# Attention exponentials tied behind the SiLU of their slot in ScalarE's order

## The chip, the cores and the metric

The kernel runs on one core of a Trainium2 chip. The metric is the device time of one execution in microseconds (us); the time of a kernel is the median of its runs. Engines are named as the profile names them: PE is TensorE, ACT is ScalarE, DVE is VectorE, POOL is GpSimd, SP is SyncE, whose queue issues the DMAs.

## The reference

Three layers, all in float32. First an attention with 4 batches, 8 heads, 576 positions and a head size of 64, in which heads 0 to 3 see the last 32 positions (local) and heads 4 to 7 see every 32nd earlier position (strided):

```python
scores = np.where(masks[None], scale * np.matmul(q, k.transpose(0, 1, 3, 2)), -1000000000.0)
attn = np.exp(scores - np.max(scores, axis=-1, keepdims=True))
attn = attn / (np.sum(attn, axis=-1, keepdims=True) + 1e-09)
x = np.matmul(attn, v)               # becomes 2304 tokens x 512
```

Then a gated layer, `y = (silu(x @ w_gate) * (x @ w_val)) @ w_out`, with 1536 inner columns, and at the end `h = max(y @ w1, y @ w2, y @ w3)` with 768 columns and `out = h @ w_out2`.

## The kernel before, in words

The float32 products are made of high and low parts: each operand is split into a rounded part (`hi`) and the rest (`lo`), and three matmuls stand for one product. The split of a value takes one copy (mostly on ACT) and one subtraction (DVE or POOL).

The 2304 tokens are cut into 5 chunks of 480 or 448 tokens, and the gated layer runs chunk after chunk. In each chunk there are 12 slots, one for each 128 inner columns, 60 slots in all, numbered 0 to 59 here. A slot is `emit_gate` (12 matmuls into `ps_g`, then the SiLU on ACT, L523, into `ht`), `emit_val` (12 matmuls into `ps_v`, the multiplication with `ht` on DVE, L530, and from the second chunk on its split into `hh` and `hl`) and, one slot later, `emit_out` (the matmuls into `ps_y`). `ps_g` and `ps_v` share a pool of two PSUM banks (tag `gv`), so the gate matmuls of one slot can begin only when the SiLU of the slot before has read its bank, and the value matmuls only when the multiplication has.

Attention of a chunk is computed while PE works on the chunk before. It comes in two kinds, and both fill `x` of the coming chunk (`xh`, `xl`):

- A `Block` uses PE for its scores (L299, L303). DVE adds the mask and takes the maximum (L311, L314), ACT takes the exponentials, two or four activations each with its row sum (L316), DVE or POOL normalize (L319 to L321), PE transposes (L326), ACT copies (L329), PE multiplies with the values (L340), and ACT and DVE split the result into `x` (L345, L346). A block's `loc` buffer and its two PSUM banks (tag `att`) are free for a later block when this is done; there are two of each.
- A `Unit` (the strided rows that don't go to PE) has its scores on POOL and DVE (`qk`, L415, L418), then a softmax on DVE and one activation on ACT (L425), its product with the values on POOL and DVE (`pv`, L437, L440), a transpose on PE (L447), and the split into `x` (L458, L459). One `stsc` and one `sto` buffer serve all units in turn.

`attention_steps` spreads these steps over the slots, and the loop over slots emits them (`fill`) behind `emit_gate` and `emit_val` of the slot. In the first 8 blocks (`early`) all comes before the first slot. In slots 0 to 43 there are 20 blocks and 10 units. Their exponentials are emitted in slots 0, 2, 4, 6, 9, 13, 21, 25, 33 and 37 (blocks, two in each) and 2, 11, 15, 19, 23, 27, 31, 35, 39 and 43 (units).

The order in which the program emits instructions isn't the order in which an engine gets them. A planner runs a simulated timeline over the program (`schedule_with_timeline_sim=True`), takes for each engine the earliest emitted instruction that is ready there, and so fixes each engine's order; on the chip each engine works through its order without overtaking. `tc.issue_after(ins)` adds an edge, without a semaphore: what is emitted inside it comes behind `ins` in the order of that engine. The kernel uses it at several places already, such as for the conversion steps of later weights (tied behind the multiplication of their slot).

The activation table of ACT holds either the exponential or the SiLU. Where one follows the other in ACT's order, a table load (`ACT_TABLE_LOAD`) stands between them, shown at the line of the activation that needs it. Copy and Abs run with either table.

After slot 59 a second stage (L570 to L700) computes the last two layers; the change doesn't touch it.

Of the kernel before, what the change touches and what calls it, by code (L numbers as in the profile page):

```python
# [11 lines left out]
AF = mybir.ActivationFunctionType  # L12
# [39 lines left out]
SCALE = 1.0 / D ** 0.5  # L52
# [7 lines left out]
def tile_attention_swiglu_maxout(  # L60
# [18 lines left out]
    nc = tc.nc  # L79
# [38 lines left out]
    def width(c):  # L118
        return STRIDE * (ROWS[c + 1] - ROWS[c])
# [125 lines left out]
    class Block:  # L245
# [59 lines left out]
        def softmax(self, norm_eng):  # L305
            sm, mx, sums, ng = self.sm, self.mx, self.sums, 2 * self.nu
            with ExitStack() as tied:
                if early_order[0] is not None and self.early:
                    tied.enter_context(tc.issue_after(early_order[0]))
                for g in range(ng):  # L310
                    nc.vector.tensor_tensor_reduce(  # L311
                        sm[:, g], self.s[:, g], self.masks[g // 2], 1.0, -3.0e38, ALU.add, ALU.max, mx[:, g:g + 1]
                    )
            early_order[0] = nc.vector.tensor_scalar(mx, mx, -SCALE, None, ALU.mult).ins  # L314
            for g in range(ng):
                nc.scalar.activation(  # L316
                    sm[:, g], sm[:, g], AF.Exp, bias=mx[:, g:g + 1], scale=SCALE, accum_out=sums[:, g:g + 1]
                )
            nc.vector.tensor_scalar(sums, sums, 1.0e-9, None, ALU.add)  # L319
            nc.vector.reciprocal(sums, sums)  # L320
            norm_eng.tensor_tensor(sm, sm, sums[:, :, None].to_broadcast([128, ng, self.nk]), ALU.mult)  # L321
# [60 lines left out]
    class Unit:  # L382
# [37 lines left out]
        def softmax(self):  # L420
            sc, n, jn = self.sc, self.n, self.jn
            mx = tiny.tile([128, 6], F32, name="smx")[:, :n]
            nc.vector.tensor_reduce(mx, sc, AX.X, ALU.max)
            nc.vector.tensor_tensor(sc, sc, mx[:, :, None].to_broadcast([128, n, jn]), ALU.subtract)
            nc.scalar.activation(sc, sc, AF.Exp, scale=SCALE)  # L425
            sums = tiny.tile([128, 6], F32, name="ssum")[:, :n]
            nc.vector.tensor_reduce(sums, sc, AX.X, ALU.add)
            nc.vector.tensor_scalar(sums, sums, 1.0e-9, None, ALU.add)
            nc.vector.reciprocal(sums, sums)
            nc.vector.tensor_tensor(sc, sc, sums[:, :, None].to_broadcast([128, n, jn]), ALU.mult)  # L430
            self.o = st_p.tile([128, 6, D], F32, name="sto")
# [75 lines left out]
    def linear(ps, w, x, n):  # L507
        xh, xl = x
        for k in range(NK):
            ks = slice(k * 128, (k + 1) * 128)  # L510
            product(ps, w[0][:, ks], w[1][:, ks], xh[:, k, :n], xl[:, k, :n], k == 0, k == NK - 1)

    hs = {}

    last_val = []
    yacc = {}

    def emit_gate(c, f):
        n = width(c)
        ps = gv.tile([128, 512], F32, name="ps_g", tag="gv")  # L520
        linear(ps[:, :n], wt["g", f], xt[c], n)
        t = h_p.tile([128, N], F32, name="ht", tag="ht" if c or f % 2 else "hh")[:, :n]
        nc.scalar.activation(t, ps[:, :n], AF.Silu)  # L523
        return t

    def emit_val(c, f, t):
# [225 lines left out]
    if True:  # L752
# [32 lines left out]
        for s, (c, f) in enumerate(slots):  # L785
# [4 lines left out]
            if work:  # L790
                weight_step()
            t = emit_gate(c, f)
            if work:
                weight_step()
# [170 lines left out]
```

## Time and profile before

| what | value |
|---|---|
| runs | 848.91, 852.14, 855.87 us; median 852.14 us |
| the profiled execution's own time | 850.72 us |
| span in its profile (first to last instruction) | 848.9 us |
| mean granted TensorE clock | 0.986 of full speed |
| PE busy | 808.7 us, 95% of the span |
| ACT busy | 374.4 us, 44% |
| DVE and POOL busy | 519.3 us (61%) and 408.7 us (48%) |

A row of the timeline has the start, the duration, the engine, the line, the operation with its output and inputs, and in brackets the engine's idle time before it and what ended that. The SiLUs of the 60 slots run in the order of the slots, so the n-th SiLU of the timeline belongs to slot n - 1, and an exponential's place among them can be read off. A row of the windows view gives, for a stretch, its length and the busy time of each engine with the number of instructions, then the granted clock (1.00 is 2.4 GHz, half of it 1.2 GHz) and the DMA's share and rate.

### The profile page before, as it was taken

What the parts mean: (1) busy time and instruction counts of PE and PEld (TensorE: products, weight loads), DVE (VectorE), ACT (ScalarE), POOL (GpSimd) and SP (SyncE); (2) the same over time, 40 slices, a digit from 0 to 9 for tenths busy, and PEclk for the clock granted to TensorE, in tenths of its full rate; (3) what the DMA queues carried; (4) which work ended last, traced back from release to release, by engine and by line L of the source; (5) the groups of instructions that cost most, each with busy time, mean ns of one, the idle gap of its engine ahead of it and who ended that gap; (6) DMA issues with size and microseconds to landing.
All of it is one profiled execution on the core that took longest, in us unless ns stands there. A gap on an engine that the chain in (4) does not pass through costs nothing.

```text
span 848.9 us, 12625 instructions
## 1 busy us (share of the span) xinstructions
PE 808.7 (95%) x4392; PEld 712.2 (84%) x4392; DVE 519.3 (61%) x1028; ACT 374.4 (44%) x844; POOL 408.7 (48%) x355
## 2 busy tenths in 40 slices
PE   4699988989999999999998999999999999999997
PEld 3577665768888899989887999999999899989986
DVE  3889977886576778846889552543644254524340
ACT  4987677653545353645243233432244123512220
POOL 0586566876477869746788444430313021302110
PEclk9799998999999999999999999999999999999999
DMA  8779688986766699868677997579766385654502
GB/s 231 237 237 363 202 273 294 361 261 215 246 201 217 220 311 313 297 194 274 205 226 212 350 300 271 169 291 407 252 234 217 129 284 215 220 190 147 212 1 75
DMA packets 73915, 202.72 MB, mean 239 GB/s; under 512 B 8716, under 2 KB 38472, under 8 KB 70268
## 3 DMA queue, kind: packets, MB, share of 16 engines
q1 hardware_dynamic: 73852, 201.92, 69.8%
q8 instruction: 35, 0.57, 0.3%
q14 instruction: 28, 0.23, 0.1%
HBM read 160.21 MB, written 41.68 MB: 238 GB/s over the span
## 4 chain that ended last, share of the span: by engine, by line
PE 63%; DVE 7%; POOL 3%; DMA 2%; issue 2%; ACT 2%; SPq 0%; DVEq 0%; ACTq 0%; POOLq 0%
PE ps_a L611 13%; PE ps_z L684 8%; PE ps_c L611 7%; PE ps_v L503 3%; PE ps_g L503 3%; PE ps_y L505 3%; PE ps_v L505 3%; PE ps_g L504 3%; PE ps_b L611 3%; PE ps_v L504 3%; PE ps_y L504 3%; PE ps_y L503 3%; PE ps_g L505 3%; POOL pr L415 1%; DMA wr<-wsdr 1%
## 5 line engine op out<-in xcount | busy, mean ns | idle before, releaser
L138 POOL TENSOR_TENSOR hl<-t,hh 128x384 fp32r<-128x384 f32 x36 | 37.6, 1047 | 207.5 <-ACT hh L135 160.4
L503 PE MATMUL ps_g<-xh,wh_g 128*128 128x448 f32 (+1 forms) x240 | 94.4, 394 | 10.2 <-ACT ht L523 8.1
L611 PE MATMUL ps_a<-yhT,wr 128*128 128x384 f32 x324 | 94.4, 338 | 0.6 <-ACT s L625 0.6
L503 PE MATMUL ps_v<-xh,w_v 128*128 128x448 f32 (+1 forms) x240 | 90.5, 377 | 3.5 <-DVE ht L530 3.3
L138 POOL TENSOR_TENSOR hl<-ht,hh 128x448 fp32r<-128x448 f32 (+1 forms) x48 | 60.1, 1253 | 68.1 <-ACT hh L135 60.7
L504 PE MATMUL ps_g<-xl,wh_g 128*128 128x448 f32 (+1 forms) x240 | 90.7, 378 | 0.9 <-DVE xl L346 0.9
L505 PE MATMUL ps_g<-xh,wl_g 128*128 128x448 f32 (+1 forms) x240 | 90.2, 376 | 0.0
L505 PE MATMUL ps_v<-xh,w_v 128*128 128x448 f32 (+1 forms) x240 | 89.5, 373 | 0.0
L504 PE MATMUL ps_v<-xl,w_v 128*128 128x448 f32 (+1 forms) x240 | 89.2, 372 | 0.0
L625 ACT ACTIVATE s<-ps_a 128x384 f32<-128x384 f32 x81 | 39.4, 490 | 98.4 <-PE ps_a L611 98.2
L437 POOL TENSOR_TENSOR pr<-stv,stsc 128x832 f32<-128x832 f32 (+17 forms) x42 | 67.5, 1625 | 29.2 <-DVE stsc L430 13.4
L415 POOL TENSOR_TENSOR pr<-stk,stq 128x832 f32<-128x832 f32 (+17 forms) x42 | 70.9, 1708 | 9.0 <-DVE sto L440 7.3
L505 PE MATMUL ps_y<-hh,w_o 128*128 128x448 f32 (+1 forms) x192 | 71.4, 372 | 0.0
L504 PE MATMUL ps_y<-hl,w_o 128*128 128x448 f32 (+1 forms) x192 | 71.2, 371 | 0.0
L160 POOL TENSOR_SCALAR raw<-raw 128x512 f32<-128x512 f32 x60 | 54.1, 902 | 33.4 <-ACT w L158 15.9
L503 PE MATMUL ps_y<-hh,w_o 128*128 128x448 f32 (+1 forms) x192 | 68.2, 374 | 0.0
L135 ACT ACTIVATE hh<-ht 128x448 fp32r<-128x448 f32 (+1 forms) x48 | 28.0, 584 | 88.4 <-DVE ht L530 88.4
L684 PE MATMUL ps_z<-wo2t,hh 128*128 128x512 f32 x216 | 64.8, 392 | 0.9 <-ACT osb L693 0.7
L530 DVE TENSOR_TENSOR ht<-ps_v,ht 128x448 f32<-128x448 f32 (+1 forms) x60 | 37.9, 631 | 41.9 <-PE ps_v L505 25.8
L503 PEld LDWEIGHTS ps_g<-xh,wh_g 128*128 128x128 f32 x240 | 45.8, 191 | 18.6 <-ACT ht L523 10.0
L611 PEld LDWEIGHTS ps_a<-yhT,wr 128*128 128x128 f32 x324 | 59.7, 188 | 1.6 <-ACT s L625 1.0
L163 DVE CUSTOM_DVE_ANT_0 w<-w,q 128x1024 uint16<-128x1024 uint16 x60 | 54.1, 902 | 1.7
(138 smaller groups left out, 1982.4 us busy)
## 6 DMA issues: line engine op xcount, KB each, us to landing
wr<-wsdr SPq DMA_DIRECT2D x27, 1792.0 KB, 7.5
raw<-in_w_dram SPq DMA_DIRECT2D x60, 512.0 KB, 5.3
w_v<-wvdr SPq DMA_DIRECT2D x48, 512.0 KB, 4.7
w_o<-wodr SPq DMA_DIRECT2D x48, 512.0 KB, 4.8
wsdr<-whi SPq DMA_DIRECT2D x27, 256.0 KB, 4.0
wvdr<-w_v SPq DMA_DIRECT2D x12, 512.0 KB, 4.5
wodr<-w_o SPq DMA_DIRECT2D x12, 512.0 KB, 5.8
wsdr<-w SPq DMA_DIRECT2D x18, 256.0 KB, 4.1
```

The lines of the kernel that those rows point to most:

```text
L138: return a.ins, lo_eng.tensor_tensor(lo, src, f32(hi), ALU.subtract).ins
L160: nc.gpsimd.tensor_scalar(f32(hi), f32(hi), -0.0, 1.0, ALU.mult, ALU.mult)
L163: nc.vector.tensor_tensor(w, w, q, ALU.add)
L415: eng.tensor_tensor(pv, self.k[:, 0:i + 1, :], self.q[:, r:r + 1, :].to_broadcast([128, i + 1, D]), ALU.mult)
L437: eng.tensor_tensor(pv, self.v[:, :, 0:i + 1], self.sc[:, r:r + 1, 0:i + 1].to_broadcast([128, D, i + 1]), ALU.mult)
L503: nc.tensor.matmul(ps, wh, xh, start=first, stop=False)
L504: nc.tensor.matmul(ps, wh, xl, start=False, stop=False)
L505: nc.tensor.matmul(ps, wl, xh, start=False, stop=last)
L530: m = nc.vector.tensor_tensor(t, ps[:, :n], t, ALU.mult).ins
L611: nc.tensor.matmul(ps, wts[:, c, a, ks], y[k][b], start=first and k == q == 0, stop=k == 1 and q == 2, skip_group_check=True,)
L625: nc.scalar.activation(s, self.a, AF.Copy)
L684: nc.tensor.matmul(z[j], a[:, ts], w[:, f, b], start=f == q == 0, stop=f == NF2 - 1 and q == 2)
```

## The change

`emit_gate` keeps its SiLU in the list `silu`, and the exponentials of blocks and units go through `exp`, which ties them behind it. For the early blocks the list is empty, and nothing is tied.

```diff
@@ Block.softmax
             for g in range(ng):
-                nc.scalar.activation(
+                exp(
                     sm[:, g], sm[:, g], AF.Exp, bias=mx[:, g:g + 1], scale=SCALE, accum_out=sums[:, g:g + 1]
                 )
@@ Unit.softmax
-            nc.scalar.activation(sc, sc, AF.Exp, scale=SCALE)
+            exp(sc, sc, AF.Exp, scale=SCALE)
@@
     last_val = []
+    silu = []
+
+    def exp(*args, **kw):
+        with ExitStack() as tied:
+            for ins in silu:
+                tied.enter_context(tc.issue_after(ins))
+            nc.scalar.activation(*args, **kw)
+
@@ emit_gate
-        nc.scalar.activation(t, ps[:, :n], AF.Silu)
+        silu[:] = [nc.scalar.activation(t, ps[:, :n], AF.Silu).ins]
         return t
```

## Rows read from the trace of the kernel before

**Rows 1.** The page's parts 1 and 2: busy time of engines; granted clock by slices

```profile
PE 808.7 (95%) x4392; PEld 712.2 (84%) x4392; DVE 519.3 (61%) x1028; ACT 374.4 (44%) x844; POOL 408.7 (48%) x355
...
PEclk9799998999999999999999999999999999999999
```

**Rows 2.** Windows view of all engines, three stretches of the gated layer

```profile
42.00:60.00 18.00, 16.32 (x64) 12.31 (x64) 17.61 (x35) 14.24 (x39) 14.43 (x12) 0.91 0.73 237
...
402.00:440.00 38.00, 37.27 (x205) 33.26 (x203) 30.56 (x34) 12.57 (x29) 32.59 (x21) 1.00 0.70 228
440.00:480.00 40.00, 35.77 (x177) 32.42 (x178) 29.63 (x36) 14.25 (x27) 25.95 (x18) 1.00 0.77 255
```

**Rows 3.** Timeline of PE: the three waits for a SiLU

```profile
121.56 0.49 PE L503 MATMUL ps_g<-xh,wh_g 128*128 128x480 f32 x1 [3.29 <-ACT ht L523]
...
188.61 0.77 PE L503 MATMUL ps_g<-xh,wh_g 128*128 128x480 f32 x1 [3.17 <-ACT ht L523]
...
440.90 0.47 PE L503 MATMUL ps_g<-xh,wh_g 128*128 128x448 f32 x1 [1.63 <-ACT ht L523]
```

**Rows 4.** Timeline of ACT around slots 0 and 1

```profile
43.13 0.36 ACT L316 ACTIVATE sm<-sm,stat 128x96 f32<-128x96 f32 x1
...
45.64 0.36 ACT L316 ACTIVATE sm<-sm,stat 128x96 f32<-128x96 f32 x1
...
46.73 1.28 ACT L523 ACT_TABLE_LOAD   x1
48.65 0.57 ACT L523 ACTIVATE ht<-ps_g 128x480 f32<-128x480 f32 x1 [0.63 <-PE ps_g L505]
...
54.09 0.57 ACT L523 ACTIVATE ht<-ps_g 128x480 f32<-128x480 f32 x1
```

**Rows 5.** Timeline of ACT: exponentials of slots 23 and 39, and the SiLUs of 22, 23, 39

```profile
262.33 0.25 ACT L425 ACTIVATE stsc<-stsc 128x48 f32<-128x48 f32 x1
...
268.97 0.57 ACT L523 ACTIVATE ht<-ps_g 128x480 f32<-128x480 f32 x1
...
274.01 0.57 ACT L523 ACTIVATE ht<-ps_g 128x480 f32<-128x480 f32 x1 [1.90 <-PE ps_g L505]
...
390.09 0.27 ACT L425 ACTIVATE stsc<-stsc 128x72 f32<-128x72 f32 x1
...
404.63 0.55 ACT L523 ACTIVATE ht<-ps_g 128x448 f32<-128x448 f32 x1 [1.78 <-PE ps_g L505]
```

**Rows 6.** Groups of ACT's instructions by line: the table loads

```profile
L523 ACT ACT_TABLE_LOAD x17 | 21.8, 1283 | 2.4 <-PE ps_g L505 2.1
...
L425 ACT ACT_TABLE_LOAD x10 | 12.8, 1283 | 9.0 <-DVE stsc L424 8.8
...
L316 ACT ACT_TABLE_LOAD x7 | 9.0, 1283 | 0.8 <-PEq L952 0.7
```

**Rows 7.** Timeline of PE: gate matmuls of slots 2 and 12, and of slot 48

```profile
60.51 0.48 PE L503 MATMUL ps_g<-xh,wh_g 128*128 128x480 f32 x1
...
172.70 0.75 PE L503 MATMUL ps_g<-xh,wh_g 128*128 128x480 f32 x1
...
477.45 0.36 PE L503 MATMUL ps_g<-xh,wh_g 128*128 128x448 f32 x1
```

**Rows 8.** Timeline of POOL: first products with the values of slot 39's unit

```profile
391.47 2.53 POOL L437 TENSOR_TENSOR pr<-stv,stsc 128x448 f32<-128x448 f32 x2 [4.50 <-DVE stsc L430]
...
406.91 2.89 POOL L437 TENSOR_TENSOR pr<-stv,stsc 128x576 f32<-128x576 f32 x2 [3.58 <-DVE sto L440]
```

**Rows 9.** Timeline of DVE: last parts of x for the second and the fifth chunk

```profile
168.36 0.40 DVE L346 TENSOR_TENSOR xl<-ps_a,xh 128x120 fp32r<-128x120 f32 x1
...
472.63 0.35 DVE L459 TENSOR_TENSOR xl<-ps_a,xh 64x192 fp32r<-64x192 f32 x1 [0.39 <-ACT xh L458]
```

**Rows 10.** Windows view of PE alone (length, busy, clock, DMA), behind the wait at 188

```profile
185.00:190.00 5.00, 1.83 (x7) 0.82 0.47 172
190.00:195.00 5.00, 5.00 (x21) 0.84 0.01 3
```

## Prediction

> **What bounds the kernel now.** I read the page's busy times first. PE is busy for 808.7 of 848.9 us, ACT for 374.4, and the granted clock is below full in a few slices only [rows 1]. PE sets the time, and a change in ACT's order is worth what it does to PE's gaps. The windows view says where these are: in the stretch from 42 to 60 us PE is busy for 16.32 of 18, from 402 to 440 for 37.27 of 38, from 440 to 480 for 35.77 of 40 [rows 2]. Then I looked in PE's timeline for waits whose releaser is the SiLU, since that is the instruction the change protects. There are three in the gated layer, of 3.29, 3.17 and 1.63 us, 8.09 in all [rows 3]. Last I compared ACT's order with the slots from which the exponentials are emitted, which tells what the tie can move at all.
>
> **What the tie moves.** Thirty batches of exponentials are tied (20 blocks, 10 units). ACT's order is the planner's order, so a batch that already stands behind its SiLU meets the new edge for nothing. By the timeline 24 of the 30 do; most blocks of the first chunk even run two or three SiLUs late. Six stand too early. The two blocks of slot 0 (8 activations, 43.13 to 46.00) come ahead of SiLU 0 at 48.65 [rows 4]. Four units do too: that of slot 23 runs at 262.33, ahead of SiLU 22, where SiLU 23 is at 274.01; that of slot 39 runs at 390.09 and SiLU 39 at 404.63 [rows 5]; those of slots 27 and 35 repeat the pattern, two and three SiLUs early. None of the three waits of PE stands behind one of these six: the exponentials ahead of the SiLUs of slots 7 and 13, at which PE waited 3.29 and 3.17, were emitted in slots 4 and 9, so the tie permits that order. I expect no direct gain.
>
> **Table loads.** One load takes 1283 ns, and there are 17 + 10 + 7 = 34 [rows 6]. The blocks of slot 0 still use the table of the early blocks; behind SiLU 0 they need a load to the exponential and one back: two more. The units of slots 23, 27 and 39 share their table period with the blocks of slots 21, 25 and 37; behind their own SiLU they stand alone: two more each. The unit of slot 35 had a pair to itself and keeps it. So 34 becomes 42, and ACT gains 8 x 1.283 = 10.3 us of 374. ACT isn't the bound, so only the place of each pair matters.
>
> **Slot 0.** Between SiLU 0 and SiLU 1 now come 8 activations (45.64 + 0.36 - 43.13 = 2.9 us) and two loads (2.6), 5.4 in all. SiLU 1 ends at 54.66 today, and the gate matmuls that need its bank start at 60.51 [rows 4, 7]: 5.85 us of cover, by PE's value and output matmuls between. The 5.4 fits, and 2.9 us of ACT's time ahead of SiLU 0 come free, so I take 0. If that cover weren't there it would cost 5.4. A gain here I leave out: ACT's vacated time lies ahead of SiLU 0, which waits for PE itself (0.63 [rows 4]). Behind the batch wait, on DVE, the row sums' reciprocals and the normalizing, then PE's transposes; through the two `loc` buffers so do SP's three loads of each block of slot 2. The exponentials start at about 48.65 + 0.57 + 1.28 = 50.5 instead of 43.13: 7.4 us late.
>
> The Trainium skill, "ScalarE: Activation LUTs", section "What ACT_TABLE_LOAD costs", puts a drain of about 1380 ns beside each load, 2.66 us a switch, and its section on table sets advises to do all calls of one set together, the opposite of this change. The trace doesn't agree: the load at 46.73 is 1.28 long and ends at 48.01, and the 0.63 from there to the SiLU is a wait for PE [rows 4]. By the page's figure the stretch ahead of SiLU 1 would be 5.4 + 2 x 1.38 = 8.2, over the cover of 5.85 by 2.3, and the sum would be that much higher; this is the last rival below.
>
> **Units of slots 23, 27 and 35.** Each moves 8 to 16 us back. None of PE's waits for a SiLU lies between 189 and 440 [rows 3], the units' turns at `stsc` and `sto` set the pace, and their rows of `x` are due a chunk boundary later. I take 0 for the three; without that cover each would cost its two loads on the path, 2.6, and 0 is the low end, since PE has nothing there to win.
>
> **Unit of slot 39.** This one goes into a loaded stretch: POOL is busy 32.59 of 38 us from 402 to 440, DVE 30.56 [rows 2]. Its exponential moves from 390.09 to about 404.63 + 0.55 + 1.28 = 406.5, 16.4 us. But the early start brought little: POOL made two products at 391.47 (2.53 us) and did the third only at 406.91, because `sto` wasn't free [rows 8]. So the products move back by those 2.5 us and by some 0.8 for DVE's four small steps, 3.3 us. The next unit (slot 43) waits for `stsc`; it fills the last columns of `x` for the fifth chunk, ready at 472.63 + 0.35 = 472.98, used by PE at 477.45 [rows 7, 9]. Slack 4.5, which 3.3 doesn't use up. The cost is then only what DVE and POOL lose in 440 to 480, where PE already misses 4.2 us [rows 2]. Lower end 0; upper end: all 16.4 less the slack of 4.5 and some 8 of POOL's idle time to 468, 3.9 us. I take 1.0, near the low end, because POOL's own rows give 3.3 against 4.5.
>
> **Sum.** 0 + 0 + 1.0 on the profiled execution's 850.7 makes 851.7. The median of the runs lies 1.4 above that execution (852.14 against 850.72), so the median after is predicted at 853.1 us, and a difference within 1%, 8.5 us (843.6 to 860.7), is about what a measurement of this kernel can't tell from none. Own range of this case: 848 to 858. Since the first move is at 43 us and the planner orders everything behind it anew, small waits of 1 to 3 us will come and go elsewhere.
>
> **Rivals.**
> - Slower: the attention of the first chunk hands the 7.4 us on. Each pair of blocks waits for the buffers of the pair before, so the lateness may travel from slot 0 to the last block of the second chunk's `x`, at 168.36 + 0.40 = 168.8. PE needs it at 172.70 [rows 7, 9]; over 3.9 us of lateness PE stands. Undiminished, that is 3.5 us of waiting. Behind the wait of 3.17 at 188 the granted clock was 0.82 and 0.84 for 10 us [rows 10], so that part of it ran at 1.2 GHz instead of 2.4: (0.18 + 0.16) x 5 = 1.7 more. Together 5.2; if the slack is gone too, 9.1. Time 857 to 863, centre 860. For it: these blocks run late by slots already. Against it: the transposes' results wait several us for their turn on PE, which absorbs part.
> - Faster: with the order laid anew from slot 0, the exponentials ahead of SiLUs 7, 13 and the copies ahead of 43 fall differently, and the waits of 8.09 us go, with the 1.7 of clock: up to 9.8, time 843 to 848. For it: these waits come from accidents of the order. Against it: the tie doesn't forbid them, and new ones are as likely.
> - The stretch from 402 to 480 is worse than I take it: all 3.9, and 1.7 of clock behind the wait, 5.6 in place of 1.0: 857.7.
> - The drain of the page: 2.3 more, 855.4. The loads of rows 6 are all 1283 ns, and the rows around them show no second piece.
>
> **Chances.** Forecast 0.52, slower by the first chain 0.20, faster by a new order 0.20, last stretch 0.06, drain 0.02. Over 1% faster: 0.13 of the faster rival's 0.20 and 0.02 from the tail of the forecast, 0.15. Over 1% slower: 0.11 of the first chain, 0.02 of the last stretch and 0.03 of the forecast's tail, 0.16. The rest, 0.69, is within 1%. The range goes from the faster rival's low end to just past the slower one's high end: 843 to 864.
>
> **What would show it.** In the profile after: about 42 table loads; no L316 or L425 ahead of its slot's SiLU, the 8 of slot 0 between SiLUs 0 and 1; gate matmuls of slot 2 with no wait for L523; those of slot 12 with none for `xl`; PE's busy time the same within 1 us, and its idle time within 5 of 40.2. I'm wrong if fewer table loads appear (then the batches merged), if PE waits at slot 2 or 12 for more than 2 us, or if the waits of rows 3 go together.

## The result and the profile after

The changed kernel is slower: 860.79 us median (859.09 to 861.39, 6 runs) against 852.68 (848.91 to 855.87, 6 runs), a ratio of 1.0101 with a 95% interval of 1.0078 to 1.0124. That is 8.1 us between the medians. The profiled execution took 859.09 us with a span of 857.3, against 850.72 and 848.9 before.

The page of the changed kernel, its part 1 (busy us, share of the span, instructions) and the granted clock of its part 2:

```profile
PE 810.4 (95%) x4392; PEld 712.0 (83%) x4392; DVE 518.1 (60%) x1028; ACT 384.7 (45%) x852; POOL 403.0 (47%) x355
...
PEclk9789999999999999999999999999999999999999
```

ACT has 10.3 us more work than in [rows 1], the 8 added table loads and nothing else. PE's work grew by 1.7 us only, so of the 8.4 us of longer span 6.7 are idle time of PE. The question is where PE stands. The windows view over all engines answers it, here first for the kernel before, in the stretches that [rows 2] leave out (length, then busy us and instructions of PE, PEld, DVE, ACT, POOL, then PE's clock, DMA share, GB/s):

```profile
60.00:110.00 50.00, 49.95 (x255) 36.23 (x255) 46.59 (x79) 35.61 (x68) 32.82 (x33) 1.00 0.84 281
110.00:150.00 40.00, 34.17 (x154) 23.55 (x154) 31.49 (x75) 30.86 (x72) 24.73 (x26) 0.91 0.85 288
150.00:203.00 53.00, 49.83 (x262) 38.18 (x261) 41.62 (x75) 27.82 (x57) 40.77 (x28) 0.97 0.77 263
203.00:402.00 199.00, 198.42 (x1096) 176.31 (x1095) 137.48 (x312) 98.31 (x225) 135.89 (x121) 1.00 0.78 257
```

The same view of the changed kernel, with the three stretches of [rows 2] as well:

```profile
42.00:60.00 18.00, 16.95 (x59) 12.78 (x60) 13.38 (x25) 14.11 (x34) 11.12 (x11) 0.81 0.58 179
60.00:110.00 50.00, 46.62 (x238) 33.26 (x237) 46.27 (x79) 34.93 (x69) 27.61 (x31) 1.00 0.80 269
110.00:150.00 40.00, 36.05 (x182) 25.61 (x181) 32.50 (x64) 28.93 (x64) 24.86 (x28) 1.00 0.85 288
150.00:203.00 53.00, 45.67 (x210) 34.16 (x209) 40.67 (x82) 30.82 (x66) 40.91 (x26) 0.97 0.79 277
203.00:402.00 199.00, 195.03 (x1095) 172.59 (x1094) 139.03 (x305) 97.16 (x212) 129.99 (x117) 0.99 0.76 247
402.00:440.00 38.00, 37.40 (x207) 33.59 (x205) 27.13 (x41) 19.15 (x43) 27.71 (x22) 1.00 0.62 207
440.00:480.00 40.00, 37.64 (x186) 33.28 (x185) 28.74 (x39) 15.42 (x29) 35.86 (x23) 1.00 0.79 250
```

PE loses 3.3 us of busy time in 60 to 110, 4.2 in 150 to 203 and 3.4 in 203 to 402, and wins 1.9 in 110 to 150 and 1.9 in 440 to 480. In the stretch around slot 0 itself, 42 to 60, PE is busy for 16.95 us against 16.32, but that isn't more work: the clock was 0.81 against 0.91, and 59 matmuls ran in place of 64. That nothing is lost there is seen from the slots: PE's last value matmul of slots 0 to 4 starts within 0.5 us of its time before. The price of the move is paid later than at the move.

**The first pass (slots 0 to 11).** PE's waits from 45 to 203 us, by what it waited for (total us, times, longest), before:

```profile
PE ps_g L503 <- ACT ht L523: 6.5, 2, 3.3
PE ps_a L303 <- DVE w L163: 2.5, 1, 2.5
```

and after (the SiLU is L531 now):

```profile
PE ps_g L503 <- ACT ht L531: 7.6, 5, 3.2
PE ps_a L326 <- DVE sm L321: 2.1, 2, 1.9
PE ps_v L505 <- DVE w_v L138: 1.5, 2, 0.8
PE ps_a L303 <- issue: 1.2, 1, 1.2
PE ps_y L557 <- DVE w L163: 1.1, 1, 1.1
PE ps_v L503 <- ACT w_v L135: 0.6, 1, 0.6
PE ps_a L340 <- issue: 0.6, 1, 0.6
```

The 9.0 us become 14.7. New are waits for weights that aren't converted yet (`w_v` and the `w` of the output matmuls L557; 3.2 us) and for the normalizing of the blocks (`sm`, L321; 2.1), and there are more, shorter waits for the SiLU. ACT's timeline at slot 0 shows where the lateness begins (start, length, engine, line, operation, output<-input, and in brackets the idle time before and its releaser):

```profile
45.04 1.28 ACT L531 ACT_TABLE_LOAD   x1
48.62 0.57 ACT L531 ACTIVATE ht<-ps_g 128x480 f32<-128x480 f32 x1 [2.30 <-PE ps_g L505]
49.21 1.28 ACT L522 ACT_TABLE_LOAD   x1
50.50 0.38 ACT L522 ACTIVATE sm<-sm,stat 128x96 f32<-128x96 f32 x1
...
53.55 0.36 ACT L522 ACTIVATE sm<-sm,stat 128x96 f32<-128x96 f32 x1
...
53.91 0.66 ACT L158 ACTIVATE w<-raw 128x512 f32<-128x512 f32 x1
...
57.90 1.28 ACT L531 ACT_TABLE_LOAD   x1
59.20 0.57 ACT L531 ACTIVATE ht<-ps_g 128x480 f32<-128x480 f32 x1
```

The eight exponentials stand between SiLU 0 and SiLU 1, as asked, with a load ahead of and behind them. But the time that they left, ahead of SiLU 0, stays empty: ACT now waits 2.30 us for PE there (0.63 in [rows 4]). And the conversions of weights that were queued behind SiLU 0 (L158, L159, L135) come later. But for one copy (L135), which stands among the exponentials, they begin with L158 at 53.91, 4.3 us later than in this row of the kernel before: 2.9 of exponentials and 1.28 of load.

```profile
49.64 0.67 ACT L158 ACTIVATE w<-raw 128x512 f32<-128x512 f32 x1
```

In the first pass DVE and PE are fed through these conversions. My reading is that when ACT is behind, each load between a batch and a SiLU counts. ACT's timeline at slot 7 has no gap in it, and PE waits for its SiLU:

```profile
117.62 1.28 ACT L522 ACT_TABLE_LOAD   x1
118.92 0.34 ACT L522 ACTIVATE sm<-sm,stat 128x60 f32<-128x60 f32 x1
...
121.56 0.61 ACT L135 ACTIVATE wh_g<-w 128x512 fp32r<-128x512 f32 x1
122.19 1.28 ACT L531 ACT_TABLE_LOAD   x1
123.48 0.57 ACT L531 ACTIVATE ht<-ps_g 128x480 f32<-128x480 f32 x1
```

```profile
124.11 0.49 PE L503 MATMUL ps_g<-xh,wh_g 128*128 128x480 f32 x1 [1.56 <-ACT ht L531]
```

At each of the five waits for a SiLU a load stands right ahead of that SiLU.

**Slot 26.** In 203 to 402 most of the loss is one wait, in PE's timeline:

```profile
312.08 0.53 PE L503 MATMUL ps_g<-xh,wh_g 128*128 128x448 f32 x1 [3.98 <-ACT ht L531]
```

Behind it the granted clock was 0.83 over 312 to 322, where it was 1.00 before, so part of that stretch ran at 1.2 GHz. ACT ran six exponentials of slot 25's blocks (307.92 to 310.18) and a load ahead of that SiLU, and had itself waited 4.45 us for their maxima from DVE. Before, these exponentials began at 299.01; they are 8.9 us late where PE is 3.5 late. DVE's timeline some 30 us earlier shows where that begins, and ACT's rows what came of it:

```profile
280.64 0.20 DVE L427 TENSOR_REDUCE ssum<-stsc 128x4 f32<-128x48 f32 x1 [5.11 <-ACT stsc L522]
...
307.92 0.38 ACT L522 ACTIVATE sm<-sm,stat 128x96 f32<-128x96 f32 x1 [4.45 <-DVE stat L314]
...
311.49 0.54 ACT L531 ACTIVATE ht<-ps_g 128x448 f32<-128x448 f32 x1
```

The row sum at 280.64 is of slot 23's unit, whose exponential is now tied behind SiLU 23. DVE takes its instructions in order, so all its other work stood for 5.11 us behind this one (1.08 us before).

That stall isn't simply handed on: behind it DVE idles again, for 1.99 and 0.81 us, for POOL's products. The rows show a second step. POOL's products with the values of slot 23's unit begin at 281.58 in place of 265.64, so the products for slot 27's unit (L415) come later too, and now run beside DVE's conversions of weights ahead of slot 25's maxima. After, on DVE and POOL:

```profile
298.52 2.50 DVE L162 SCALAR_TENSOR_TENSOR w<-w,raw 128x512 int32<-128x512 int32 x1
...
298.07 5.36 POOL L415 TENSOR_TENSOR pr<-stk,stq 128x1024 f32<-128x1024 f32 x2
```

And before, where POOL stood idle:

```profile
294.83 0.68 DVE L162 SCALAR_TENSOR_TENSOR w<-w,raw 128x512 int32<-128x512 int32 x1
...
297.34 1.15 POOL L138 TENSOR_TENSOR hl<-ht,hh 128x448 fp32r<-128x448 f32 x1 [4.09 <-ACT hh L135]
```

The conversions (L161 to L163) between slots 23 and 26 take DVE 10.2 us in the changed kernel and in the two experiments below that tie slot 23's unit and keep the SiLU, and 5.2 before and in the experiments that tie only slot 0 or only slot 27. These 5 us are about what slot 25's exponentials are late by beyond PE's own lateness (5.4). No run tests this step by itself.

To see when the lateness arises I took the start of PE's last value matmul (L503) of each slot, after less before: about 0 up to slot 4, +4.4 us at slot 7, −0.6 at slot 10 (a wait of before falls away), +4.5 from slot 14 to 22, +3.5 at slots 24 to 26, +9.3 at slots 27 to 40, +6.0 at slot 45, +9.2 from slot 49 to the end. The middle of these steps is uncertain: kernels whose order of instructions is that of before up to slot 22 (in two of them with loads added) lag there by −3.4 to +3.2 us, one execution each. So the parts are settled by medians, in the experiments.

### The profile page after: what moved, and what is told of

Same layout as the page of the kernel before. It is cut to its first block, busy times and chain, and to the rows that moved or that the text cites. A ratio compares the mean times of both kernels' runs of the same rounds, so it can differ in the third digit from the quotient of the medians.

```text
span 857.3 us, 12645 instructions
## 1 busy us (share of the span) xinstructions
PE 810.4 (95%) x4392; PEld 712.0 (83%) x4392; DVE 518.1 (60%) x1028; ACT 384.7 (45%) x852; POOL 403.0 (47%) x355
## 4 chain that ended last, share of the span: by engine, by line
PE 69%; DVE 8%; ACT 7%; DMA 6%; POOL 5%; issue 4%; SPq 1%; ACTq 0%; DVEq 0%; POOLq 0%
PE ps_a L619 13%; PE ps_z L692 8%; PE ps_c L619 7%; PE ps_g L503 4%; PE ps_g L504 4%; PE ps_g L505 4%; PE ps_v L503 4%; PE ps_y L505 4%; PE ps_v L505 4%; PE ps_y L504 4%; PE ps_y L503 4%; PE ps_v L504 4%; PE ps_b L619 3%; DVE w L162 2%; DVE w L163 2%
## 5 line engine op out<-in xcount | busy, mean ns | idle before, releaser
L503 PE MATMUL ps_g<-xh,wh_g 128*128 128x448 f32 (+1 forms) x240 | 94.7, 394 | 14.4 <-ACT ht L531 12.3
L503 PE MATMUL ps_v<-xh,w_v 128*128 128x448 f32 (+1 forms) x240 | 90.1, 376 | 2.2 <-DVE ht L538 1.5
L415 POOL TENSOR_TENSOR pr<-stk,stq 128x832 f32<-128x832 f32 (+17 forms) x42 | 71.5, 1715 | 6.2 <-DVE stat L314 2.9
L135 ACT ACTIVATE hh<-ht 128x448 fp32r<-128x448 f32 (+1 forms) x48 | 28.1, 585 | 95.8 <-DVE ht L538 92.5
L160 POOL TENSOR_SCALAR raw<-raw 128x512 f32<-128x512 f32 x60 | 49.7, 830 | 42.6 <-issue 25.7
L503 PE MATMUL ps_y<-hh,w_o 128*128 128x448 f32 (+1 forms) x192 | 66.9, 376 | 0.0
L503 PEld LDWEIGHTS ps_g<-xh,wh_g 128*128 128x128 f32 x240 | 46.4, 193 | 23.7 <-ACT ht L531 15.2
L162 DVE SCALAR_TENSOR_TENSOR w<-w,raw 128x512 int32<-128x512 int32 x60 | 55.8, 930 | 7.8 <-POOL raw L160 5.3
```

The costliest lines, as they stand in the source:

```text
L160: nc.gpsimd.tensor_scalar(f32(hi), f32(hi), -0.0, 1.0, ALU.mult, ALU.mult)
L162: nc.vector.scalar_tensor_tensor(w, w, 3, hi, ALU.logical_shift_left, ALU.bitwise_xor)
L415: eng.tensor_tensor(pv, self.k[:, 0:i + 1, :], self.q[:, r:r + 1, :].to_broadcast([128, i + 1, D]), ALU.mult)
L503: nc.tensor.matmul(ps, wh, xh, start=first, stop=False)
```

## Experiments

Ratios are to the kernel before, run in the same job on the same chip. A ratio on record isn't the quotient of the two medians; where the two differ by a microsecond or more, both are given. Theory T: the loss is that of slot 0's tie (work on ACT behind it is delayed) and that of slot 23's tie, each by itself. Its rivals: the new order as a whole, or the eight loads by their number.

**Only slot 0 tied; only the units; only slot 23; only slot 27.** In the changed kernel the exponentials are tied only where the slot is in a list; in the four runs it is `(0,)`, `(23, 27, 35, 39)`, `(23,)` and `(27,)`:

```diff
-        silu[:] = [nc.scalar.activation(t, ps[:, :n], AF.Silu).ins]
+        silu[:] = [ins for ins in [nc.scalar.activation(t, ps[:, :n], AF.Silu).ins]
+                   if c * NF + f in (0,)]
```

> Only the two blocks of slot 0 are tied. Theory A (the lateness comes in two places, slots 0 to 13 and the SiLU of slot 26): this part alone makes the gate of slot 14 about 4.5 us later than before and brings no wait at slot 26, so the time is 3 to 5 us over before. Rival B (each added pair of table loads costs its 2.6 us): two loads more, 2.6 us or less. Rival C (only the order being laid anew counts, and parts don't add up): any time within 6 us of before, with waits at other places than in the changed kernel.

Measured: 860.02 us (5 runs) against 851.58, ratio 1.0081 (1.0051 to 1.0112). The medians differ by 8.4 us, the ratio gives 6.9; either is more than the 3 to 5 expected. PE has no wait at slot 26 here.

> Only the units of slots 23, 27, 35 and 39 are tied. Theory A: no lateness up to slot 22; the SiLU of slot 26 behind waiting exponentials, PE standing 3 to 4 us there and some 1.8 us of clock; about 3.6 us won back at slot 45; in all 3 to 5 us over before. Rival B: six loads more, 7.7 us or less. Rival C: within 6 us of before, the wait at slot 26 not there.

Measured: 855.15 us (10 runs), ratio 1.0037 (1.0013 to 1.0061).

> Only the unit of slot 23 is tied. Theory A in its sharper form (DVE stands 5 us for the row sums of this unit, its conversions come later, and the exponentials of slot 25 come late in front of SiLU 26): PE waits 3 to 4 us at slot 26 or 27 already with this tie alone, 4 to 6 us over before. Rival (the unit of slot 27 is needed for it): no wait there, within 1 us of before.

Measured: 856.78 us (10 runs), ratio 1.0061 (1.0037 to 1.0085). The wait at slot 26 is there by this tie alone. DVE and PE of this kernel:

```profile
272.67 0.20 DVE L427 TENSOR_REDUCE ssum<-stsc 128x4 f32<-128x48 f32 x1 [5.73 <-ACT stsc L522]
...
304.10 0.74 PE L503 MATMUL ps_g<-xh,wh_g 128*128 128x448 f32 x1 [3.96 <-ACT ht L531]
```

Lag against before steps by 6.6 us from slot 26 to 27. The wait is 3.96 of it, and the granted clock behind it, 0.50 over 304 to 309, about 2: twelve matmuls start 0.37 us apart there, 0.20 at full clock. This kernel has 38 loads, four more than before: slot 27's unit, late now too, no longer shares its table with slot 25's blocks.

> Only the unit of slot 27 is tied. Theory A, sharper form: no wait at slot 26, within 2 us of before. Rival (this unit's place decides, since without it the table of slot 25's exponentials is loaded only behind the value multiplication): the wait of 3 to 4 us at slot 26 appears here, 4 to 6 us over before.

Measured: 851.36 us (10 runs), ratio 1.000 (0.9974 to 1.0026), and no wait at slot 26. The same sort of tie costs nothing here.

What follows: slot 0's tie alone costs 0.81%, the units 0.37%; together 1.18% against the 1.01% of the whole change, the same within the intervals, which are wide (by the medians it is 12.0 us against 8.1). Slot 23 alone (0.61%) costs more than the four units together by its median, which suggests that the late units give something back. That the planner lays the whole order anew falls as an explanation. In the traces the order of DVE, ACT and POOL with slot 23 tied alone is that of before up to 258 us; with slot 0 tied alone it is that of the changed kernel up to 270 us; and with only the four units tied it is that of the changed kernel from 290 us on. The changed order is made of these local moves.

**The late units alone.** The same edit with `(27, 35, 39)`.

> Only the units of slots 27, 35 and 39 tied: the change without the two ties that cost. If slots 0 and 23 are the whole cost, this is within 2 us of before, with the wait of 3.3 us at slot 45 gone and some of it given back at slot 48. Rival: the parts don't add, and it is 4 us or more over before.

Measured: 850.08 us (846.8 to 851.64, 10 runs) against 852.5, ratio 0.997 (0.9949 to 0.999). This is faster than both kernels, by about 2.5 us against before, just beyond the 2 us expected. PE's waits in 440 to 480, of before and then of this kernel:

```profile
PE ps_v L503 <- DVE ht L530: 3.3, 1, 3.3
PE ps_g L503 <- ACT ht L523: 1.6, 1, 1.6
```

```profile
PE ps_v L503 <- DVE ht L538: 0.9, 1, 0.9
PE ps_a L447 <- DVE sto L440: 0.9, 1, 0.9
PE ps_y L504 <- POOL hl L138: 0.8, 1, 0.8
PE ps_g L503 <- ACT ht L531: 0.7, 1, 0.7
```

The wait of 3.3 goes, 4.9 us in all become 3.3. Some 1.6 us of the 2.5 are seen here; the two profiled executions end alike (850.58 and 850.72 us), so they don't show the rest. Slot 27 cost nothing by itself; 35 and 39 were not separated.

**The order without the loads.** SiLU is replaced by the exponential, so that ACT keeps one table throughout (one load in the run); the order of DVE, ACT and POOL stays as it is, by the traces. Done to the kernel before, to slot 0's tie alone, and to the changed kernel:

```diff
-        nc.scalar.activation(t, ps[:, :n], AF.Silu)
+        nc.scalar.activation(t, ps[:, :n], AF.Exp)
```

> The kernel before with the exponential in place of the SiLU (the SiLU is left out), so that one table serves all and 33 of the 34 table loads go; the planner's order is the same. Theory L (table loads in front of SiLUs are on PE's path): the waits of PE at slots 7 and 13 shrink by 1.3 to 2.6 us each, 4 to 8 us under before. Theory O (only the order of the waits for DVE counts): under 3 us.

Measured: 847.24 us (10 runs), ratio 0.9949 (0.9935 to 0.9963).

> Only the blocks of slot 0 tied, and the exponential in place of the SiLU (the SiLU is left out): no table loads after the first, order as in the run with slot 0 alone tied. Compared with the kernel before without table loads. Theory L: the 8.4 us of slot 0's tie shrink to 3 us or less, since the two loads ahead of SiLU 1 delay the conversions of later weights. Theory O: 6 to 9 us remain, from exponentials and conversions standing in another order.

Measured: 849.26 us (10 runs), ratio 0.9972 (0.9953 to 0.9991).

> The changed kernel with the exponential in place of the SiLU (the SiLU is left out): 41 of 42 loads go, order as changed. Compared with the kernel before without table loads. Theory L: within 3 us of it, and the wait of PE at slot 26 falls from 4.0 to 1.5 us or less. Theory O: 7 to 9 us over it, with the wait at slot 26 at 2.7 us or more (4.0 less the 1.3 of the load back).

Measured: 847.48 us (10 runs), ratio 0.995 (0.9931 to 0.9968).

Without loads the changed kernel and the kernel before take the same time, 847.48 and 847.24 us. All loads together cost about 0.5% before (ratio 0.9949 to 1) and 1.5% in the changed kernel (0.995 to 1.0101). Slot 0's tie keeps about a quarter of its price without them, 0.23% or 2.0 us; as the whole change keeps 0.2 us, the units' ties must win back some 1.8 there, which is a difference and not a run. In PE's waits from 45 to 203 us with slot 0's tie alone the SiLU no longer appears, the weights and the normalizing do; the longest:

```profile
PE ps_a L326 <- DVE sm L321: 3.0, 1, 3.0
PE ps_v L505 <- DVE w_v L138: 1.7, 2, 1.2
PE ps_a L303 <- DVE xl L346: 1.2, 1, 1.2
PE ps_y L557 <- DVE w L163: 1.2, 1, 1.2
```

The time of the changed kernel without loads is as theory L had it. At slot 26, though, it still waits, 2.81 us in place of 3.98, as theory O had it. The 1.17 less is nearly the 1.283 of one load, such as the one ahead of the SiLU; but all loads are out in this run. The granted clock behind the shorter wait stayed at 1.00 (305 to 315).

**Which loads.** Slot 0 tied, and the exponential in place of SiLU in slot 0 only, which takes out the two added loads there and leaves the order as it is:

```diff
-        silu[:] = [nc.scalar.activation(t, ps[:, :n], AF.Silu).ins]
+        silu[:] = [ins for ins in [nc.scalar.activation(t, ps[:, :n],
+                   AF.Silu if c + f else AF.Exp).ins] if c + f == 0]
```

> Only the blocks of slot 0 tied, and in slot 0 alone the exponential stands in place of the SiLU (that SiLU is left out): the two added loads between 45 and 51 us go, the order on every engine stays that of the run with slot 0 alone tied. Theory L0 (the two loads there, handed on through the conversions of weights, make most of its 8.4 us): 1 to 4 us over before. Rival (the loads of the later slots, or the order, make it): 6 to 9 us over before.

Measured: 855.89 us (7 runs) against 850.08, ratio 1.0067 (1.004 to 1.0094). This lies between the two theories, just under the rival's 6 to 9 us. The two loads of slot 0 are not the main price: 5.8 us stay.

The other way round, the kernel before with the exponential in slot 1, which adds two loads between SiLU 0 and SiLU 2 without moving anything:

```diff
-        nc.scalar.activation(t, ps[:, :n], AF.Silu)
+        nc.scalar.activation(t, ps[:, :n], AF.Exp if c * NF + f in (1,) else AF.Silu)
```

> The kernel before, in its own order, with the exponential in place of the SiLU in slot 1 alone (that SiLU is left out), which adds two table loads, ahead of that activation and ahead of SiLU 2. Theory L0 (any two loads in this stretch are handed on): 3 to 8 us over before. Rival (it takes the 8 exponentials behind SiLU 0 as well): under 2 us over before.

Measured: 851.25 us (12 runs) against 850.08, ratio 1.0005 (0.9986 to 1.0024). Two loads in that place, without the moved exponentials, cost nothing that shows.

Then eight added loads in quiet slots of the kernel before, the same edit with `(17, 29, 50, 55)`:

> The kernel before, in its own order, with the exponential in place of the SiLU in slots 17, 29, 50 and 55 (these SiLUs are left out), which adds eight table loads, as many as the change does, where ACT waits for PE and no conversions hang on it. If only the place of a load counts: within 1.5 us of before. If loads cost by their number: 8 to 10 us over before.

Measured: 852.55 us (12 runs) against 850.08, ratio 1.0013 (0.9992 to 1.0034), 1.1 us by the ratio and 2.5 by the medians. The number of loads, 42 as in the changed kernel, is not the price either.

Last, slot 0 tied with the exponential in slots 1 to 13, which leaves 22 loads, and the order as it is:

```diff
-        silu[:] = [nc.scalar.activation(t, ps[:, :n], AF.Silu).ins]
+        silu[:] = [ins for ins in [nc.scalar.activation(t, ps[:, :n],
+                   AF.Exp if 0 < c * NF + f < 14 else AF.Silu).ins] if c + f == 0]
```

> Only the blocks of slot 0 tied, and in slots 1 to 13 the exponential in place of the SiLU (these SiLUs are left out): the load ahead of SiLU 0 and the one behind it stay, those of slots 1 to 13 go, the order stays. Theory L1 (with the conversions 4 us late, the loads of the following slots lie on PE's path, and cost more than the two added ones): 1 to 3 us under before, since before pays for its own loads in these slots too. Rival (the lateness comes from order and from the load behind SiLU 0): 4 us or more over before.

Measured: 853.53 us (12 runs) against 851.42, ratio 1.0018 (0.9998 to 1.0038). This lies between what the two theories said. It stands 2.1 us over before by the medians (1.5 by the ratio). The lag at slot 22 in the profiled executions falls in the same order: +7.4 us with slot 0 tied, +3.4 without the loads of slot 0, −0.3 without those of slots 1 to 13. That run isn't a clean subtraction, though, and its 2.1 us can't be set beside the 2.0 above, which are counted from a kernel without loads. Before has SiLU waits at loads in these slots too [rows 3], and the kernel before without the loads of slots 1 to 13 was not run. If these were worth anything up to the 0.5% of all loads, slot 0's tie would keep 0.2 to 0.7% in this run.

## Why the prediction was wrong in its steps and right in its range

The median was forecast at 853.1 us, no change to speak of, with 843 to 864 as the range. It came out at 860.79, in the range but outside the 848 to 858 of the forecast's own case, and at the edge of what was called "within 1%" (843.6 to 860.7). The case that came true in size is the slower rival (857 to 863, centre 860), though not by its mechanism, and only part of the loss in its place. That the range held is luck: it reached so far for a reason that didn't come true.

**The signs.** The loads, the order and slots 2 and 12 came out as listed. PE's busy time did not stay within 1 us (1.7 more), nor its idle time within 5 of 40.2 (46.9). None of the three signs of being wrong appeared, and yet the forecast was nearly 8 us short: they watched the places that the forecast had already thought of.

**What the tie moves: right.** Six of thirty batches move. All exponentials stand behind their SiLU.

**Table loads: right in number, half right in their worth.** 42 were forecast and the profile has 42, ACT's busy time is 10.3 us up as worked out. The groups of ACT's loads by line are these:

```profile
L522 ACT ACT_TABLE_LOAD x21 | 26.9, 1283 | 6.4 <-DVE stsc L424 3.9 <-DVE s L198 1.4 <-PEq L960 0.7
L531 ACT ACT_TABLE_LOAD x21 | 26.9, 1283 | 9.4 <-PE ps_g L505 9.2
```

"Only the place of each pair matters" is what the eight loads in quiet slots showed (0.13%, 0 within the interval). But I looked at the place of the added ones only. Moving slot 0's batch raised the price of loads that were there already: its tie costs 0.67% with the two added loads out and 0.23% with all loads out.

**Slot 0, "I take 0": this step failed.** The cover that it counted on was there: SiLU 1 ends at 59.77, and slot 2's gate matmuls start at 60.57 without a wait. What I left out is what else is queued on ACT behind the exponentials, the conversions of the weights of the next slots, and how late the blocks' own normalizing would come; PE waits for both in the rows above. I also wrote that 2.9 us of ACT's time ahead of SiLU 0 "come free". They did, and stayed idle; on an in-order engine nothing that stands behind SiLU 0 could use them. The term that I set at 0 measured 0.81%, about 6.9 us (8.4 by the medians): some 2 by the order alone, the rest only together with the table loads, and mostly not the two added ones. The split holds to 2 us or so.

**The slower rival: right place for slot 0's part, another carrier.** I let the lateness travel through the attention's buffers to `x` of the second chunk, due at slot 12. The last part of that `x` came at 172.66 + 0.38 = 173.0, 4.3 us late, and slot 12's gate matmuls, six of which had run at 169.77, went on at 176.17 without a wait for it. PE lost its time before that, at weights, at SiLUs and for 1.9 us at the normalizing of the blocks.

**Units of slots 23, 27 and 35, "I take 0 for the three": failed for slot 23.** 27 is 0, as taken. Slot 23 costs 0.61%, 5.2 us, twice the upper bound of 2.6. That bound counted two loads of its own for the unit. I argued that none of PE's waits for a SiLU lies in that stretch, which said what could be won there and nothing on what could be lost. The tied exponential made DVE's row sum wait and POOL's products come later; DVE's conversions, now beside them, took 10.2 us in place of 5.2; and slot 25's exponentials came late, just ahead of SiLU 26. That the tie of slot 23 makes the wait is shown by its own run, the steps between are read from rows.

**Slot 39, +1.0: right in its small size, wrong in sign.** The exponential runs at 415.83; forecast were 406.5, and with the 9.3 us by which the whole kernel is late there that is the same. PE then lost less in 440 to 480 than before, 2.4 us against 4.2, and the late units alone (27, 35 and 39 together) are a small gain.

**The faster rival** rested on an order laid anew from slot 0 on. The orders meet again each time, so its reason fell. Of its three waits [rows 3] slot 13's stayed (3.19), slot 7's fell to 1.56 and that of 440.90 went; with it went a wait of 3.3 behind it, and the late units won from that.

**The Trainium skill's drain** ("ScalarE: Activation LUTs", section "What ACT_TABLE_LOAD costs") is not seen after either: the load at 49.21 is 1.28 us long and the next exponential starts at 50.50. But that page's advice to do all calls of one set before switching (section "Table sets: the hidden batching unit" and the rules at its end) would have pointed to the right side: without the two sets in turn the changed order costs nothing, 847.48 against 847.24 us.

## What to carry to other kernels

When an instruction moves back on an in-order engine, its own consumer is only the first thing to look at: list everything queued behind it on that engine, then on the engine that will wait for it in order, and then what work will newly run beside what. Price a table load by its place: eight added loads cost 0.13%, not clear of nothing, where the engine has slack, and one moved batch, slot 0's, cost 0.67% with its own two loads out and 0.23% with none left. A tie that most of the work already meets can be kept where it was measured to pay (here the units of slots 27, 35 and 39) and left off elsewhere.

## What was not expected of the hardware

A table load that stands between a late batch and a SiLU seems to pass almost whole into PE's wait: 3.98 us with it, 2.81 with all loads out. DVE's conversion L162 takes 0.66 to 0.69 us wherever POOL is idle beside it, and 2.50 beside POOL's products L415 at slot 25; why is not shown. One kernel's executions differ more than the parts sought here: the kernel before ran from 848.43 to 855.23 us in 31 runs, and by slot 22 executions with one order of instructions are already some 3 us apart either way. A ledger of two profiled executions says where time may have gone, and only medians said how much. What stays open: how slot 0's price splits between the delayed conversions, the later blocks and the loads, beyond these 2 us; what slot 23's tie costs without loads, which was not run; and whether slot 35 or slot 39 wins the 0.3%.
